# Splitting the output stores of the first two batches into two transfers each

## The chip, the cores and the metric

The kernel runs on one core of one Trainium2 chip. A core has a matrix engine (TensorE, PE in the profile), VectorE (DVE), ScalarE (ACT), GpSimd (POOL) and SyncE (SP). All of them work on the on-chip memory SBUF; TensorE's results go to banks of a second memory, PSUM. Transfers between SBUF and the device memory (DRAM) run on 16 DMA engines that the core's engines share; an engine only issues a transfer, in its own order of instructions, and goes on. Here SP issues the stores and the transposing transfers, and GpSimd issues nearly all loads. Completion of a transfer reaches those who wait for it through semaphores.

The metric is the device time in microseconds (us), the median of several runs.

## The reference

Attention through 32 memory slots per head, followed by a gated feed-forward block:

```python
a = softmax(phi, axis=2)                       # over the 576 positions, for each memory slot
k_m = einsum('bhsm,bhsd->bhmd', a, k)          # 32 x 64 for each batch and head
v_m = einsum('bhsm,bhsd->bhmd', a, v)
scores = (1 / sqrt(64)) * q @ k_m.transpose(0, 1, 3, 2)
attn_out = softmax(scores, axis=-1) @ v_m      # (8, 8, 576, 64)
x = attn_out.transpose(0, 2, 1, 3).reshape(4608, 512)
g = x @ w_gate                                 # 512 -> 1536
out = (g / (1 + exp(-g)) * (x @ w_val)) @ w_out    # 1536 -> 512, float32
```

There are 8 batches of 576 tokens. The output is 4608 x 512 floats, 9.44 MB.

## The kernel before

The kernel works batch by batch. For each batch, TensorE forms the sums over positions, the scores, the gate and value products (line 508), and the last product with `w_out` (line 719). That last product is computed with seven block products in place of eight (a scheme with sums of blocks). Each batch's first 512 tokens are treated as two sets of 256, the even and the odd ones of the output (`r` below), each in two groups `u` of 128 tokens. The remaining 64 tokens of every batch are collected and stored apart ("leftover").

The output view and the store. One call writes 256 tokens: partition `t` of the tile holds two rows of output, for `u` = 0 and 1.

```python
out_r = out.rearrange("(b t r) c -> b r t c", b=B, r=2)
...
def store_block(t_o, b, n, cols):
    nc.sync.dma_start(
        out=out_r[b, n, 0:256, cols].rearrange("(u t) c -> t u c", u=2), in_=t_o[:, :, cols]
    )
```

The tiles that are stored come from a pool with three buffers in rotation (tag `to`); a buffer can be written again when the store that read it has landed:

```python
work = ctx.enter_context(tc.tile_pool(name="work", bufs=3))
...
def add(out, home, other, free=False):              # line 749, VectorE
    nc.vector.tensor_tensor(out=out, in0=mine[home], in1=mine[other], op=ALU.add)
    if free:
        done(mine[home])                            # gives the PSUM bank back

def both(name, t0, cols):
    store_block(mine[name], b, t0 // 256, cols)

def c11():
    t = tile_of("o1", (128, 2, DM), tag="to")       # DM = 512 columns, lo and hi are its halves
    add(t[:, :, lo], "a", "p1", True)
    if end:                                         # end: the last batch alone
        both("o1", 0, lo)

def c22():
    t = tile_of("o2", (128, 2, DM), tag="to")
    add(t[:, :, hi], "s", "p5")

def c12():
    t = mine["o1"]
    add(t[:, :, hi], "c", "q6", True)
    both("o1", 0, hi if end else slice(0, DM))      # the even tokens' store

def c21():
    t = mine["o2"]
    copy("v" if end else "a", t[:, :, lo], mine["s"])
    done(mine["s"])
    both("o2", 256, slice(0, DM))                   # the odd tokens' store
```

So batches 0 to 6 have two stores of 512 KB each. Both halves of a tile are finished by one instruction, the addition in `c12` or the copy in `c21`.

On the same queue of SP are the transposing transfers of q and, for later batches, of the small matrices `t_bkv`:

```python
def load_qT(b):
    qTs[b] = att.tile([128, NS, 128], BF16, tag="qT", name="t_qT")
    nc.sync.dma_start_transpose(out=qTs[b], in_=qs[b])      # line 117
```

The loads of a batch are issued by GpSimd, three batches ahead (batch 4's once batch 1's last products are under way):

```python
def loads(b):
    if b < B:
        load_q(b)
        load_phi(b, nc.gpsimd)
        load_k(b)
        load_v(b)
```

The order of issue is fixed by hand. Batches 0 and 1 are the first two; their last products and their four stores come together, at the start of the loop over the batches from 2 on:

```python
(zero, ops0), (one, ops1) = products(0, ("c11",)), products(1, ("p1", "c11"))
...
run(zero[12:16] + zero[18:22] + kv[1:] + q2[2:] + zero[16:18] + zero[22:24])
...
loads(4)
backlog = one[6:12] + zero[36:] + one[12:36]
```

Of the kernel before, what the change touches and what calls it, by code (L numbers as in the profile page):

```python
# [14 lines left out]
def kernel(  # L15
# [19 lines left out]
    nc = tc.nc  # L35
# [29 lines left out]
    out_r = out.rearrange("(b t r) c -> b r t c", b=B, r=2)  # L65
# [604 lines left out]

    def store_block(t_o, b, n, cols):

        nc.sync.dma_start(
            out=out_r[b, n, 0:256, cols].rearrange("(u t) c -> t u c", u=2), in_=t_o[:, :, cols]
        )

    def store_leftover(t_o, b, cols, eng):

# [2 lines left out]
    def products(b, by_hand, quad=None):  # L681
# [71 lines left out]
        def both(name, t0, cols):  # L753
            store_block(mine[name], b, t0 // 256, cols)
# [354 lines left out]
```

The softmax here doesn't subtract the row's maximum and nothing guards it: scores larger than these inputs give would overflow.

## Time and profile before

| What | Number |
|---|---|
| median of three runs | 235.75 us (235.49 to 235.82) |
| span of the profiled execution | 233.8 us |
| granted TensorE clock, mean | 0.998 |
| TensorE busy | 224.5 us (96%) |
| VectorE, ScalarE, GpSimd busy | 78%, 74%, 60% |
| DMA | 36.84 MB in 36610 packets, mean 158 GB/s |
| stores of 512 KB, line 673 | 15, median 3.8 us from issue to landing |
| stores of 256 KB, line 673 | 2, median 2.2 us from issue to landing |

How to read it. Times are counted from the first instruction of the profiled execution. "Busy" is the time in which an engine works at an instruction; matmuls are pipelined, and a busy TensorE is not by that alone at its peak. The page cuts the span into 40 equal slices and gives each engine's busy share in tenths; the DMA row is the mean busy share of the 16 DMA engines. A row of "busy times by stage" has the stage, its length, then for each engine its busy time and in brackets its instructions (PE, weight loads, DVE, ACT, POOL), the granted clock, the DMA share and GB/s. An issue of a transfer in the SP queue is short; the time "to landing" runs from the issue to the last semaphore event of the transfer. The chain is the sequence of work that ended last, followed back from the end.

### The profile page before, as it was taken

The numbers are of one execution on the slowest core, as the hardware profiler recorded it, in microseconds if no ns is written. First come the engines' busy times: TensorE is split into PE (matmuls) and PEld (weight loads), VectorE is DVE, ScalarE is ACT, GpSimd is POOL, SyncE is SP. The second block draws the span as 40 slices with busy tenths as digits, with TensorE's granted clock in tenths as the row PEclk, the third lists the DMA queues.
The fourth block names the chain that finished last, engine by engine and source line by source line (L and its number), as shares of the span: only waits on it lengthen the run. The fifth ranks groups of instructions, "written<-read, shape, count | busy, mean of one in ns | idle before, by whom it ended". The sixth has DMA issues, their size and how long they took to land.

```text
span 233.8 us, 7201 instructions
## 1 busy us (share of the span) xinstructions
PE 224.5 (96%) x2825; PEld 169.9 (73%) x2825; DVE 183.2 (78%) x421; ACT 173.5 (74%) x369; POOL 140.6 (60%) x190
## 2 busy tenths in 40 slices
PE   7997899999999999999999999999999999999992
PEld 2554466778887776878788787877788778878881
DVE  4056799999966698989797767999799879977732
ACT  2759798988547889968896658968897789677220
POOL 8422536998199059665966688464745494039390
PEclk9999999999999999999999999999999999999999
DMA  6999999999995993999199946995024502201224
GB/s 213 210 210 206 200 206 207 231 236 266 205 241 134 261 251 47 231 227 151 35 259 212 190 128 121 254 217 94 15 78 110 106 0 94 90 35 57 62 76 136
DMA packets 36610, 36.84 MB, mean 158 GB/s; under 512 B 14560, under 2 KB 30944, under 8 KB 36576
## 3 DMA queue, kind: packets, MB, share of 16 engines
q0 software_dynamic: 16272, 22.42, 51.5%
q1 hardware_dynamic: 19536, 13.18, 23.6%
q10 hardware_dynamic: 768, 0.79, 1.1%
q8 instruction: 22, 0.36, 0.6%
q14 instruction: 12, 0.10, 0.1%
HBM read 42.47 MB, written 9.44 MB: 222 GB/s over the span
## 4 chain that ended last, share of the span: by engine, by line
PE 88%; DMA 7%; POOL 1%; ACT 1%; DVE 1%; issue 1%; POOLq 0%
PE p_v L508 21%; PE p_g L508 21%; PE p_os L719 20%; PE p_oc L719 10%; DMA t_kv<-in_v_dram 7%; PE p_u L465 5%; PE p_oa L719 5%; PE p_kv L230 2%; PE p_g L389 1%; POOL t_kv L99 1%; PE p_mT L318 1%; PE p_warm L866 1%; PE p_q L376 0%; POOL t_q L108 0%; DVE t_kT L332 0%
## 5 line engine op out<-in xcount | busy, mean ns | idle before, releaser
L531 DVE TENSOR_TENSOR t_h<-t_sg,p_v 128x288 bf16<-128x288 bf16 x192 | 81.9, 452 | 17.3 <-PE p_v L508 7.4
L508 PEld LDWEIGHTS <-t_U 128*128 128x128 bf16 x768 | 73.6, 98 | 23.2 <-issue 3.8
L525 ACT ACTIVATE t_sg<-p_g 128x288 bf16<-128x288 f32 x192 | 74.0, 424 | 17.8 <-PE p_g L508 11.5
L508 PE MATMUL p_g<-t_A,t_U 128*128 128x288 bf16 x384 | 77.1, 286 | 0.5 <-ACT t_U L487 0.5
L508 PE MATMUL p_v<-t_A,t_U 128*128 128x288 bf16 x384 | 77.2, 286 | 0.0
L719 PEld LDWEIGHTS <-t_S 128*128 128x128 bf16 x384 | 37.5, 98 | 4.5 <-issue 0.2
L596 POOL TENSOR_TENSOR t_S<-t_h 128x512 bf16<-128x512 bf16 x17 | 19.6, 1155 | 32.5 <-DVE t_h L531 30.4
L719 PEld LDWEIGHTS <-t_h 128*128 128x128 bf16 x288 | 27.1, 98 | 8.6 <-issue 5.0
L485 ACT CAST t_U<-p_u 128x512 bf16<-128x512 f32 x53 | 28.0, 607 | 6.6 <-PE p_u L465 6.6
L719 PE MATMUL p_os<-t_T,t_S 128*128 128x256 bf16 x192 | 23.7, 273 | 0.0
L553 POOL TENSOR_TENSOR t_S<-t_S,t_h 128x512 bf16<-128x512 bf16 x17 | 19.6, 1154 | 1.3
L553 POOL TENSOR_TENSOR t_S<-t_h,t_S 128x512 bf16<-128x512 bf16 x16 | 18.4, 1151 | 0.0
L553 POOL TENSOR_TENSOR t_S<-t_h 128x512 bf16<-128x512 bf16 x16 | 18.4, 1150 | 0.0
L465 PE MATMUL p_u<-W,t_kT 64*32 64x512 bf16 (+1 forms) x416 | 15.8, 364 | 0.6 <-DVE t_kT L332 0.6
L866 PE MATMUL p_warm<-bones 128*128 128x512 bf16 x44 | 13.8, 457 | 1.7 <-DVE bones L888 1.7
L719 PE MATMUL p_os<-t_T,t_h 128*128 128x256 bf16 x96 | 14.8, 273 | 0.0
L489 DVE CAST t_U<-p_u 128x512 bf16<-128x512 f32 x19 | 12.4, 684 | 1.9 <-PE p_u L465 1.9
L445 DVE TENSOR_TENSOR t_A<-t_E,t_lz 128x576 bf16<-128x576 bf16 x16 | 11.4, 739 | 0.7 <-ACT t_lz L421 0.7
L719 PE MATMUL p_oc<-t_T,t_S 128*128 128x256 bf16 x96 | 12.0, 273 | 0.0
L719 PE MATMUL p_oa<-WO,t_h 128*128 128x256 bf16 x96 | 11.8, 273 | 0.0
L719 PE MATMUL p_oc<-WO,t_S 128*128 128x256 bf16 x96 | 11.8, 273 | 0.0
L719 PE MATMUL p_os<-WO,t_h 128*128 128x256 bf16 x96 | 11.8, 273 | 0.0
(106 smaller groups left out, 308.8 us busy)
## 6 DMA issues: line engine op xcount, KB each, us to landing
out_dram<-t_o SPq DMA_DIRECT2D x15, 512.0 KB, 3.8
t_kv<-in_k_dram POOLq DMA_DIRECT2D x8, 576.0 KB, 10.2
t_q<-in_q_dram POOLq DMA_DIRECT2D x8, 576.0 KB, 8.6
t_kv<-in_v_dram POOLq DMA_DIRECT2D x8, 576.0 KB, 14.9
t_phi<-in_phi_dram POOLq DMA_DIRECT2D x6, 576.0 KB, 8.3
WO<-in_moe_w_out_dram POOLq DMA_DIRECT2D x3, 512.0 KB, 19.3
W<-in_moe_w_gate_dram POOLq DMA_DIRECT2D x2, 512.0 KB, 16.4
W<-in_moe_w_val_dram POOLq DMA_DIRECT2D x2, 512.0 KB, 16.2
```

Of the source, the lines that this page charges most:

```text
L230: nc.tensor.matmul(p[g][32 * i:32 * i + 32, 0:n], lhsT=phi_of(b, g, j, i), rhs=kvs[b][64 * g:64 * g + 64, w0:w1, i, j * D:(j + 1) * D], st ...
L445: nc.vector.tensor_tensor(out=a, in0=es.pop((b, g)), in1=lzs.pop((b, g)), op=ALU.mult)
L465: nc.tensor.matmul(p[g][32 * i:32 * i + 32, o:o + n], lhsT=kTs[b][64 * g:64 * g + 64, 2, 32 * i:32 * i + 32], rhs=w_part(w, c, i, g, halve ...
L485: nc.scalar.copy(out=t, in_=p)
L489: nc.vector.tensor_copy(out=t, in_=p)
L508: nc.tensor.matmul(p[:, 0:HALF], lhsT=Us[b, c, g][:, o // 2, which, 128 * (o % 2):128 * (o % 2 + 1)], rhs=atts[b, g][:, r], start=(g == 0) ...
L525: nc.scalar.activation(out=sg, in_=gate[:, 0:HALF], func=AF.Silu)
L531: nc.vector.tensor_tensor(out=dst, in0=sg, in1=val[:, 0:HALF], op=ALU.mult)
L553: eng.tensor_tensor(out=out, in0=x, in1=y, op=ALU.subtract)
L596: eng.tensor_tensor(out=t[:, 0], in0=A21, in1=A22, op=ALU.add)
L719: nc.tensor.matmul(mine[home][:, u], lhsT=lhs(c, m, u), rhs=rhs(c, m), start=fresh and u == 0, stop=(k == 5), skip_group_check=u == 1 or n ...
L866: nc.tensor.matmul(p[:, 0:128 * a], lhsT=bones, rhs=x.to_broadcast([128, a, 128]) if a > 1 else bones, start=True, stop=True,)
```

## The change

Stores of batches 0 and 1 are issued as two transfers of 128 tokens (256 KB) each, one for each `u`, in place of one of 256 tokens (512 KB). Batches 2 to 7 keep theirs. The tokens, the columns and the tiles are the same. It is meant to hand the DMA engines smaller pieces in the part of the kernel where loads for later batches run beside these stores.

```diff
     def store_block(t_o, b, n, cols):
 
-        nc.sync.dma_start(
-            out=out_r[b, n, 0:256, cols].rearrange("(u t) c -> t u c", u=2), in_=t_o[:, :, cols]
-        )
+        rows = out_r[b, n, 0:256, cols].rearrange("(u t) c -> t u c", u=2)
+        parts = [slice(u, u + 1) for u in range(2)] if b < 2 else [slice(0, 2)]
+        for u in parts:
+            nc.sync.dma_start(out=rows[:, u], in_=t_o[:, u, cols])
```

## The prediction

> **What bounds the kernel now.** I read the page first, then the engines' busy times by stage, then the chain that ended last around the four stores that the change splits, then the output tensor, the SP queue and the loads that share the DMA engines with those stores.
>
> From the page, the busy shares and the slices:
>
> ```profile
> PE 224.5 (96%) x2825; PEld 169.9 (73%) x2825; DVE 183.2 (78%) x421; ACT 173.5 (74%) x369; POOL 140.6 (60%) x190
> ...
> PE   7997899999999999999999999999999999999992
> ...
> DMA  6999999999995993999199946995024502201224
> ```
>
> TensorE is busy nearly always. The DMA row is just as full until about slice 23, so it could look like a second bound; that has to be decided stage by stage. The busy times by stage, from the first of these stores to near the end:
>
> ```profile
> 67.00:107.00 40.00, 39.95 (x565) 31.09 (x563) 34.24 (x75) 31.87 (x67) 25.21 (x33) 1.00 0.91 200
> 107.00:150.00 43.00, 42.97 (x522) 33.67 (x521) 34.45 (x78) 34.29 (x78) 33.09 (x44) 1.00 0.86 167
> 150.00:200.00 50.00, 50.00 (x656) 39.29 (x655) 44.43 (x98) 42.56 (x91) 28.54 (x40) 1.00 0.41 91
> 200.00:230.00 30.00, 29.34 (x267) 24.26 (x264) 20.92 (x45) 14.94 (x34) 15.55 (x22) 1.00 0.23 78
> ```
>
> After the length, the first column is TensorE's busy time. It is idle for 0.05, 0.03, 0.00 and 0.66 us: 0.74 us in all after the first store is issued. Busy matmuls overlap, so this alone doesn't show that they run at their rate. The chain in the same stage does:
>
> ```profile
> 65.62 1.31 PE p_os L719 x12
> ...
> 68.24 1.31 PE p_os L719 x12
> ...
> 77.07 0.49 PE p_g L508 x4
> ```
>
> Twelve products of 256 columns take 1.31 us, 109 ns each; four of 288 columns take 0.49 us, 122.5 ns each.
>
> **What the Trainium skill says.** "TensorE: Matmul & The Clock Gate", section Back-to-back issue gap, gives columns / 2.4 + 2.5 ns for a warm matmul by itself: 109.2 and 122.5 ns. The trace has the same two numbers, so TensorE is at that rate here, beside the stores. "DMA: Bandwidth & Descriptors", section Issuing engines are not separate DMA queues, says that transfers from all issuing engines run on the same 16 DMA engines and interleave. The trace agrees in part: during the third store the loads move too (below). The same page, section Anatomy of one DMA, puts a transfer issued by GpSimd at about 2.0 us plus bytes / 436 GB/s; my estimate from it is 3.2 us for 512 KB and 2.6 us for 256 KB. The quiet stores here, which SP issues, landed in 3.3 us (512 KB) and 2.2 us (256 KB, from the page's list of issues), so most of a small store is latency, and two issued together overlap it. "Perfetto Trace Analysis", section Identifying Dependency Chains, says that an instruction that waits on several others may get extra semaphore instructions ahead of it. The trace has 20 of them at the additions of line 749, mostly 21 to 50 ns.
>
> **The change, part by part.** Batches 0 and 1 each end with two stores (c12 and c21) of 128 partitions x 2 x 512 floats, 512 KB. The SP queue and the busy times around them:
>
> ```profile
> 61.32 5.97 SPq L117 DMA_TRANSPOSE t_qT<-t_q  x1
> 67.34 33.99 SPq L673 DMA_DIRECT2D out_dram<-t_o  x5
> 101.45 5.93 SPq L117 DMA_TRANSPOSE t_qT<-t_q  x1
> ```
>
> ```profile
> 71.10:74.30 3.20, 3.20 (x32) 2.87 (x31) 1.44 (x3) 3.18 (x4) 3.20 (x5) 1.00 0.61 172
> 74.30:83.20 8.90, 8.85 (x181) 6.02 (x179) 7.05 (x17) 7.08 (x18) 1.34 (x2) 1.00 0.98 237
> 83.20:90.00 6.80, 6.80 (x77) 4.94 (x75) 6.53 (x17) 5.91 (x16) 5.53 (x6) 1.00 0.96 193
> 90.00:92.00 2.00, 2.00 (x18) 1.47 (x16) 1.32 (x4) 2.00 (x6) 1.92 (x3) 1.00 0.00 0
> ```
>
> The 33.99 us is from the first of five issues to the end of the last, not busy time. The output tensor's own view, taken in narrow windows, has the issues at 67.34, 70.19, 74.30, 77.81 and 100.96 us, and 3.7, 3.3, 8.9, 8.9 and 6.4 us to landing. The first four are split; the fifth is of batch 2.
>
> Removed: 4 transfers of 512 KB. Added: 8 of 256 KB. Bytes stay at 4 x 512 KB = 2 MB, in runs of 2 KB, over the same 128 partitions. Only the order changes (all first halves, then all second halves, of each tile).
>
> 1. SP: one issue is 0.37 us, 0.58 us for the first. With the gap to the next instruction (0.05 to 0.12 us between the transposes and their neighbours) I take 0.45 us for an extra one: 4 x 0.45 = 1.8 us. SP's next other work is at 100.96 us, 22.8 us after the last of the four issues. On the path: 0.
>
> 2. Landing: both halves become ready together, since the addition or copy that finishes a tile writes both, so nothing starts earlier. The second half is issued 0.45 us later and moves half the bytes; the last byte lands, I estimate, between 0.3 us earlier and 0.6 us later than now. In the loaded stage (third and fourth store) the same bytes share the same engines, so I allow 1 us.
>
> 3. Buffers of t_o, three in rotation. The first store's buffer is rewritten by c22 of batch 1 at 74.86 us; its landing is 67.34 + 3.7 = 71.04, a slack of 3.8 us. The second's is rewritten at 96.58 and has landed at 70.19 + 3.3 = 73.5: 23 us. The third's at 100.85, landed at 74.30 + 8.9 = 83.2: 17 us. None of this is eaten by 1 us. The rewriting instruction has two completions to await instead of one: 4 x 21 to 50 ns = 0.1 to 0.2 us on VectorE, which has 40 - 34.24 = 5.8 us idle in this stage. On the path: 0.
>
> 4. Loads of batch 4, issued by GpSimd from 72.83 us, collide with the third and fourth store. They land at 79 (q), 81 (phi), 87 (k) and 90 us (v), from their issue plus 6.2, 7.9, 12.8 and 15.0 us. First uses: the phi exponential at 97.3, q's transpose at 101.45, the k and v sums at 103.87. The least slack is 103.87 - 89.9 = 14 us. The row 90 to 92 settles it: DMA share 0.00. The engines have drained everything before batch 5's loads begin at 92.01, so a different order before 90 us can't reach later transfers unless it lasts 2 us longer.
>
> Sum on the path: 0 + 0 + 0 + 0. Predicted 235.75 us, the time before.
>
> **The rivals.** First, a gain: smaller transfers let the loads through sooner, or free t_o sooner. For it speaks that the DMA engines are 98% busy from 74.3 to 83.2 us, and that a store takes 8.9 us there against 3.3 in quiet. Against it: TensorE waits for no transfer in this stage and idles 0.05 us in 40. Even if all its later idle time went, the time would be 235.75 - 0.74 = 235.0 us, 0.3%.
>
> Second, a loss at the buffer with the least slack: if the first store's second half landed 3.8 us later than now, c22 of batch 1 would stall VectorE, the PSUM bank p_os would come free late, and TensorE would wait. A doubled latency (3.7 to 7.4 us) still ends at 74.74, just ahead of 74.86. A stall of 1 to 2 us would make 236.7 to 237.7 us. Nothing in the trace suggests such a delay: the DMA share from 71.1 to 74.3 us is 0.61, so there was room.
>
> Third, a loss through the DMA engines: eight completions in place of four lengthen the drain past 92 us and push batch 5's loads. That needs 2 us or more, and these have slack of their own. I give it less weight; it would make some tenths of a us, about 236.0.
>
> **Range and chances.** The three runs before spread over 0.33 us (235.49 to 235.82). Shifts in which queue is served first can, by my judgement, move a program by as much again, so I take 235.3 to 236.3 us, with more room above, since splitting can only add instructions and the gain is capped at 0.74. Two per cent is 4.7 us: a gain of that size exceeds all idle time that TensorE has left after the change, and a loss would need several of the slacks above to fail at once. Chances: faster 0.01, same 0.98, slower 0.01.
>
> **What would show it.** In the changed profile I expect: 21 issues of line 673 in place of 17, the pairs about 0.45 us apart; halves landing in 2 to 3.5 us for the first two tiles and within about 1 us of 8.9 for the other two; the addition at 74.86 us and the transpose at 101.45 within 0.2 us of their places; TensorE busy 39.9 of 40 us from 67 to 107; DMA share near 0.00 from 90 to 92. The prediction is wrong if VectorE waits for out_dram at line 749, if the sums of batch 4 wait for a load, if the drain lasts beyond 92 us, or if matmuls lose their 109 and 122.5 ns while the stores run.

## The result, and the profile after

The changed kernel takes 235.02 us (234.82 to 235.12), against 235.78 us (235.49 to 236.11) for the kernel before, measured beside it: a ratio of 0.9966, 95% interval 0.9953 to 0.9978. It is faster by 0.76 us, 0.34%. The prediction was 235.75 us, in a range of 235.3 to 236.3; the result lies below it.

The page of the kernel after: busy shares and slices.

```profile
PE 223.6 (96%) x2825; PEld 169.7 (73%) x2825; DVE 183.2 (79%) x421; ACT 173.6 (74%) x369; POOL 140.6 (60%) x190
...
PE   7987899999999999999999999999999999999993
...
DMA  6999999999995992999099945995022702102125
```

TensorE is busy 0.9 us less, but the first slices already differ, in its warm-up. The busy times by stage of the kernel after, with the stages of the prediction:

```profile
67.00:107.00 40.00, 39.95 (x564) 31.09 (x563) 34.22 (x75) 31.91 (x67) 25.14 (x33) 1.00 0.92 200
107.00:150.00 43.00, 42.97 (x523) 33.67 (x521) 34.44 (x78) 34.30 (x77) 33.13 (x44) 1.00 0.86 167
150.00:200.00 50.00, 50.00 (x656) 39.31 (x654) 44.42 (x98) 42.55 (x91) 28.46 (x40) 1.00 0.42 91
200.00:230.00 30.00, 29.29 (x266) 24.22 (x264) 20.85 (x45) 14.89 (x34) 15.56 (x22) 1.00 0.23 78
```

The first three rows have TensorE's numbers of before to the hundredth. So has the chain, three entries of which stand here: 109 and 122.5 ns for each matmul, and each entry 0.05 or 0.06 us earlier than before.

```profile
65.57 1.31 PE p_os L720 x12
...
68.19 1.31 PE p_os L720 x12
...
77.01 0.49 PE p_g L508 x4
```

Compared matmul by matmul over the whole trace, TensorE is ahead by 0.06 us at 25.9 us and by 0.05 at 226.4, and by 0.05 or 0.06 everywhere between. The 67 to 90 us with the split stores win and lose nothing.

The SP queue of the kernel after, and the stages around the stores:

```profile
61.40 5.99 SPq L117 DMA_TRANSPOSE t_qT<-t_q  x1
67.44 33.84 SPq L676 DMA_DIRECT2D out_dram<-t_o  x9
101.39 6.26 SPq L117 DMA_TRANSPOSE t_qT<-t_q  x1
```

```profile
71.10:74.30 3.20, 3.20 (x32) 2.88 (x30) 1.44 (x3) 3.18 (x4) 3.20 (x5) 1.00 0.62 169
74.30:83.20 8.90, 8.85 (x181) 6.02 (x180) 7.04 (x17) 7.08 (x18) 1.27 (x2) 1.00 0.99 240
83.20:90.00 6.80, 6.80 (x76) 4.94 (x75) 6.52 (x17) 5.91 (x16) 5.58 (x6) 1.00 0.93 187
90.00:92.00 2.00, 2.00 (x17) 1.47 (x16) 1.32 (x4) 2.00 (x6) 1.92 (x4) 1.00 0.00 0
```

There are nine issues in place of five, and the engines have again drained by 90 us. Where, then, are the 0.7 us of the span? After all engines have stopped computing. The last stages of the kernel before:

```profile
229.00:230.00 1.00, 0.34 (x4) 0.06 (x1) 0.51 (x2) 0.00 (x0) 0.00 (x0) 1.00 0.34 80
230.00:233.80 3.80, 0.00 (x0) 0.00 (x0) 0.00 (x0) 0.00 (x0) 0.00 (x0) 0.86 0.37 86
```

and of the kernel after:

```profile
229.00:230.00 1.00, 0.29 (x3) 0.01 (x1) 0.45 (x2) 0.00 (x0) 0.00 (x0) 1.00 0.38 92
230.00:233.10 3.10, 0.00 (x0) 0.00 (x0) 0.00 (x0) 0.00 (x0) 0.00 (x0) 1.00 0.43 101
```

From VectorE's last copy on, both kernels have the same work, and it takes 3.80 us in place of 4.44, 0.64 us less. With the 0.05 us that TensorE was ahead this is the whole difference of the two spans, 233.82 and 233.13 us. What SP waited for from 229 us to the end, before and after:

```profile
SPq L1104 <- DMA out_dram<-t_q: 1.6, 2, 1.0
SPq L1104 <- PEq L1104: 0.7, 2, 0.5
```

```profile
SPq L1105 <- DMA out_dram<-t_q: 0.9, 2, 0.7
SPq L1105 <- PEq L1105: 0.7, 2, 0.5
```

At the end SP waits, one after the other, until every transfer of the kernel has landed; then come drains (instructions without a transfer) and a barrier, at which all engines meet. The SP and ACT transfers (ACT issues one early load, and three stores of 64 tokens near the end) take turns on eight semaphores, and SP's closing instructions wait for these in a fixed order. There are 44 such transfers before and 48 after. So the last one signals on the fourth semaphore before and on the eighth after. Here are the closing instructions in the two traces: their number in SP's own stream, counted from 0, the start in us, the time in ns since the instruction before ended, and which of the eight semaphores the wait holds. (The first line holds semaphores of GpSimd's loads alone.)

```
before                               after
72 230.377   46  loads               78 230.340   44  loads
73 231.385  980  first               79 230.828  460  first
74 231.446   33  second              80 230.911   55  second
75 232.088  614  third  (last, ACT)  81 230.985   47  third
76 232.183   67  fourth (last, SP)   82 231.047   34  fourth
77 232.258   47  fifth               83 231.361  286  fifth
78 232.328   42  sixth               84 231.423   34  sixth
79 232.815  459  seventh             85 232.148  697  seventh (last, ACT)
80 232.899   56  eighth              86 232.209   33  eighth  (last, SP)
81 232.969   42  drain               87 232.274   37  drain
```

"Last" marks the semaphores on which the kernel's very last two stores signal. ACT's lands last, at 232.07 us before and 232.13 after; SP's lands at 231.8 in both. Two things differ. Before, four more waits follow these two, 0.07 to 0.08 us apart but for the pause, although what they wait for has landed; after, none does. And ahead of instruction 79, in both, SP pauses for 0.46 us although what it waits for has long come: before, this stands behind the last landing; after, six instructions earlier in the ending, where SP has to wait for landings anyhow. From the wait for SP's last store, at which both have landed, to the drain it is 232.969 - 232.183 = 0.786 us before and 232.274 - 232.209 = 0.065 us after: 0.72 us. The pause is 0.459 - 0.047 = 0.41 of it, the four waits the other 0.31. Counted from VectorE's last copy, that wait is reached 0.08 us later than before, which leaves the 0.64 us.

That gave the theory for the experiments. A: the time is won in SP's closing waits, by where the last stores' semaphores stand and where the pause falls; that stores were split is beside the point. B, the change's own purpose: smaller stores let the loads pass.

### The profile page after: what moved, and what is told of

Same layout as the page of the kernel before. It is cut to its first block, busy times and chain, and to the rows that moved or that the text cites. A ratio compares the mean times of both kernels' runs of the same rounds, so it can differ in the third digit from the quotient of the medians.

```text
span 233.1 us, 7210 instructions
## 1 busy us (share of the span) xinstructions
PE 223.6 (96%) x2825; PEld 169.7 (73%) x2825; DVE 183.2 (79%) x421; ACT 173.6 (74%) x369; POOL 140.6 (60%) x190
## 4 chain that ended last, share of the span: by engine, by line
PE 88%; DMA 7%; POOL 1%; ACT 1%; DVE 1%; issue 1%; POOLq 0%
PE p_v L508 21%; PE p_g L508 21%; PE p_os L720 21%; PE p_oc L720 10%; DMA t_kv<-in_v_dram 7%; PE p_u L465 5%; PE p_oa L720 5%; PE p_kv L230 2%; PE p_g L389 1%; POOL t_kv L99 1%; PE p_mT L318 1%; PE p_warm L867 1%; PE p_q L376 0%; POOL t_q L108 0%; DVE t_kT L332 0%
## 5 line engine op out<-in xcount | busy, mean ns | idle before, releaser
L867 PE MATMUL p_warm<-bones 128*128 128x512 bf16 x44 | 13.0, 434 | 1.7 <-DVE bones L889 1.7
```

The lines of the kernel that those rows point to most:

```text
L867: nc.tensor.matmul(p[:, 0:128 * a], lhsT=bones, rhs=x.to_broadcast([128, a, 128]) if a > 1 else bones, start=True, stop=True,)
```

## The experiments

"Beside" is the kernel before, run on the same chip; "tail" is the time from the start of VectorE's last copy to the end, in the trace.

| Run | us | Beside | Ratio (95%) | Tail, us |
|---|---|---|---|---|
| before | 235.78 | | | 4.44 |
| the change | 235.02 | 235.78 | 0.9966 (0.9953 to 0.9978) | 3.80 |
| e1 small loads on SP | 235.19 | 235.85 | 0.9976 (0.9969 to 0.9983) | 3.80 |
| e2 two drains | 235.70 | 235.85 | 0.9992 (0.9984 to 1.0) | 4.44 |
| e3 six drains | 235.46 | 235.85 | 0.9984 (0.9977 to 0.999) | 3.98 |
| e4 small loads on ACT | 235.10 | 235.85 | 0.9966 (0.9953 to 0.9979) | 3.70 |
| e5 split 2, 3 | 235.05 | 235.89 | 0.9967 (0.9954 to 0.9979) | 3.78 |
| e6 split 0 to 3 | 235.57 | 235.89 | 0.9984 (0.9976 to 0.9993) | 4.18 |
| e7 change and small loads | 235.45 | 235.89 | 0.9982 (0.9975 to 0.9988) | 4.10 |
| e8 e4, one less on SP | 235.31 | 235.89 | 0.9979 (0.9969 to 0.9989) | 4.17 |
| e9 e4, two less on SP | 236.33 | 235.92 | 1.002 (1.0013 to 1.0027) | 4.26 |
| e10 e4 again | 234.93 | 235.92 | 0.9958 (0.9945 to 0.9971) | 3.71 |
| e11 e8 again | 235.41 | 235.92 | 0.9973 (0.9963 to 0.9983) | 4.17 |

**Four more transfers, no store split (e1).**

```diff
+    def tick(eng):
+        t = consts.tile([128, 4], FP32, ...)          # nobody reads it
+        eng.dma_start(out=t, in_=phi[0, 0, 0:128, 0:4])
 ...
     def store_block(t_o, b, n, cols):
         nc.sync.dma_start(...)                          # as before
+        if b < 2:
+            tick(nc.sync)
```

> The stores of batches 0 and 1 stay whole; after each of the four, SP issues a load of 2 KB that nobody reads. Theory A (the time is won at the end: SP's closing waits for the eight completion semaphores of the SP and ACT transfers come in a fixed order; four more transfers move the last stores from the third and fourth of these semaphores to the last two, and six more instructions of SP move its pause of 0.46 us from after the last landing to before it): 235.0 us, and SP's pause stays ahead of its 80th instruction, now the first but one of the closing waits. Theory B (smaller stores beside the loads win the time): 235.75 us.

235.19 us: a gain of 0.66 us, nearly that of the change, with work added and no store changed. The tail is 3.80 us as in the change, and SP's ending looks the same, pause ahead of its instruction 79 included. B falls as the main cause.

**The length of SP's stream alone (e2, e3).** Drains use no transfer, so the semaphores stay where they were. Six is the number of instructions by which the change lengthens SP's stream: four issues and two semaphore instructions.

```diff
     load_phi(0, nc.sync)
+    for _ in range(6):           # e2: 2
+        nc.sync.drain()
```

> The kernel before, with two more instructions of SP (drains, no transfer) right after its first load. Theory A: the pause of 0.46 us moves ahead by two waits, to the one on the fifth semaphore, still behind the last landing (fourth): 235.75 us, no change. A rival A2 (any instruction more on SP helps, in proportion): a third of the whole gain with six, 235.6 us. Theory B: 235.75 us.

> The same with six drains, as many instructions as the change adds to SP, and no transfer. Theory A: the pause stands ahead of the first of the eight waits, before the last landing, and is hidden; the order of the semaphores stays, so four waits of about 0.07 us follow the last landing as before: gain 0.41 us, 235.35 us. Theory B: 235.75 us.

Two drains give 0.15 us, which is hardly told from nothing (the interval reaches 1.0), and leave the tail at 4.44 us; six give 0.39 us and a tail of 3.98. In e2's trace the pause of 0.474 us is ahead of the fifth semaphore's wait, behind the last landing; in e3's no pause is left behind it, and four quick waits follow, as foreseen. So it isn't that each instruction helps: what counts is on which side of the last landing the pause falls.

**The semaphores alone (e4).** Four small loads on ACT, late, leave SP's stream as long as before.

```diff
         if last:
+            for _ in range(4):
+                tick(nc.scalar)
             rest, rest_ops = products(b, (), 1)
```

> The kernel before, with four loads of 2 KB issued by ACT in the last batch. SP's stream keeps its length, so its pause stays ahead of the same closing wait (the seventh semaphore); but the last stores now signal on the last two semaphores. Theory A: the pause falls before the last landing and is hidden, and no wait follows it: 235.05 us. If only the number of SP's instructions counted: 235.75 us. Theory B: 235.75 us.

235.10 us, and 234.93 the second time (e10): the whole gain. SP's instruction 79 is the seventh wait, as before, but now the last landing is what it waits for, and the pause is lost in that wait: the gap ahead of it is 0.619 us, against 0.697 ahead of the same wait in the changed kernel, where no pause is due.

**Splitting elsewhere, and more of it (e5, e6, e7).**

```diff
-        parts = [slice(u, u + 1) for u in range(2)] if b < 2 else [slice(0, 2)]
+        parts = [slice(u, u + 1) for u in range(2)] if b in (2, 3) else [slice(0, 2)]   # e5
+        parts = [slice(u, u + 1) for u in range(2)] if b < 4 else [slice(0, 2)]         # e6
```

e7 is the changed kernel with e1's four loads.

> The same splitting, but of the stores of batches 2 and 3 in place of 0 and 1: four more transfers, four more instructions of SP. Theory A (the gain lies in SP's closing waits: which semaphores the last stores signal on, and where SP's pause of 0.46 us falls): the last two semaphores, and the pause ahead of the third of the eight closing waits, before the last landing: 235.05 us, as for the change itself. Theory B (smaller stores beside the loads of batches 3 and 4 win the time, at 67 to 90 us): nothing is split there, so 235.8 us.

> The change doubled: the stores of batches 0 to 3 are split, eight more transfers. Eight is the number of the semaphores, so the last stores are back on the third and fourth: four waits of 0.07 us follow the last landing again. SP's pause is still away from the closing waits, now at the last store but one of SP, which it can delay by some 0.1 to 0.2 us at the end. Theory A: the gain shrinks to 0.25 to 0.45 us, 235.45 us. Theory B: twice the gain, or at least all of it: 234.3 to 235.05 us.

> The changed kernel, with the four loads of 2 KB of the first experiment added on SP. Stores of batches 0 and 1 are split as in the change, but with eight more transfers in all the last stores are back on the third and fourth semaphore, and the pause falls at the last store but one of SP. Theory A: 235.45 us, part of the gain lost. Theory B: 235.05 us, the gain stays.

Splitting the stores of batches 2 and 3 gives the same as those of 0 and 1. Doubling the change doesn't double the gain but leaves less than half of it, 0.32 us (e6); adding four loads to the change leaves 0.44 us (e7): with eight more transfers the last stores are on the third and fourth semaphore again. In e6 the pause stands ahead of the issue of SP's last store but one (0.461 us), and SP's last issue begins at 230.10 us, against 229.83 in the change, with its tail 0.38 us longer.

**The pause put back (e8 to e11).** e4's loads, and one or two leftover stores near 140 us moved from SP to ACT, so that SP has one or two instructions fewer.

```diff
-            engs = (nc.sync, nc.scalar if end and name != "c11" else nc.sync)
+            engs = (nc.sync, nc.scalar if (end and name != "c11")
+                    or (not end and name == "c12") else nc.sync)        # e9: in ("c12", "c21")
```

> The fourth experiment (four small loads on ACT, last stores on the last two semaphores), and one store of 64 tokens of batch 0 to 3 issued by ACT in place of SP, near 140 us, so that SP has one instruction fewer. SP's pause then stands ahead of the very last closing wait, behind the landing that ends the one before it. Theory A: the pause is exposed again, 235.1 + 0.41 = 235.5 us. Theory B, or a theory in which only the order of the semaphores counts: 235.1 us.

> As the eighth experiment, with a second store of 64 tokens of batches 0 to 3 issued by ACT, so that SP has two instructions fewer than in the fourth. Theory A: SP's pause stands ahead of its first closing drain, behind all eight waits, and is exposed: 235.5 us, 0.4 us more than the fourth experiment, and the last landing is no later. In the trace the stretch from the last matmul to the end is 0.4 to 0.5 us longer than there. If only the order of the semaphores counts: 235.1 us. Theory B: 235.8 us.

> The fourth experiment once more, beside the other two on one chip: 235.1 us, pause hidden.

> The eighth experiment once more, beside the other two on one chip: 235.5 us by theory A, pause exposed ahead of the last wait; 235.1 us if only the order of the semaphores counts.

e8 came out between the two expectations, so e4 and e8 were run again on one chip: 234.93 us (e10) and 235.41 us (e11), 0.48 us apart, with A's 0.41 foreseen. The end of e10's and then of e11's trace, by the span and the last copy:

```profile
core 0 of [0], span 233.3 us
...
229.56 0.42 DVE L332 COPY t_q<-p_os 128x256 f32<-128x256 f32 x1 [0.30 <-PE p_os L726]
```

```profile
core 0 of [0], span 233.2 us
...
229.07 0.42 DVE L332 COPY t_q<-p_os 128x256 f32<-128x256 f32 x1 [0.29 <-PE p_os L726]
```

The profiled execution of e11 reached its last copy 0.48 us sooner and yet ended at nearly the same time: 3.71 us of tail in e10, 4.17 in e11. In e11's, SP's pause (0.473 us) is ahead of the eighth wait, behind the landing that ends the seventh.

The two parts of the gain can now be told apart by the tail. With neither moved it is 4.44 us (before); with the pause alone moved ahead of the last landing 3.98 (e3); with the last stores alone on the last semaphores 4.17 (e11); with both 3.71 (e10). Alone they save 0.46 and 0.27 us, together 0.73, their sum. In time e11 is 0.51 us faster than before, more than its tail accounts for; in its trace TensorE was 0.31 us ahead at 25.9 us already.

e9 missed its expected 235.5 by 0.8 us. Its pause is where A puts it (0.479 us ahead of the first drain, tail 4.26 us), 0.55 us of tail more than e10. But the second moved store has a price of its own: TensorE falls behind by 0.6 us between 141.6 and 149.3 us and doesn't catch up, in e9 alone. The trace fits a delay by the issue itself: ACT issues the second moved store from 141.87 to 142.37 us, and its next pair of activations begins at 142.41, against 141.45 in e10. No run tests it. e9's time therefore says little about the pause; its trace agrees with it.

No version beats the change beyond its uncertainty: e4 and e5 are level with it.

## Why the prediction was wrong

**What bounds the kernel** was right: matmuls kept their 109 and 122.5 ns, and no experiment but e9 moved TensorE's course after the first 26 us by more than 0.12 us. None of the four signs of being wrong appeared: they all belong to the stages before 107 us, and what went wrong lies behind 230.

**Step 1, SP.** The cost of an extra issue was sized about right: the added issues took 0.42, 0.44, 0.64 and 0.45 us without the gap behind them, against 0.45 with it. But six instructions came to SP's stream, not four: two semaphore instructions follow the third and the fourth pair. The step failed in "On the path: 0". I asked only when SP was wanted next, at 100.96 us, and not whether SP is on the path at the end. It is: in the last 3.8 us, when no engine computes any more. There SP's stream is the critical path, and a longer stream with other semaphores changed it. The missing term is -0.72 us in the two traces: -0.41 by the pause (e3 gained 0.39 by it alone) and -0.31 by the waits after the last landing.

**Step 2, landing.** The halves of the first tile landed at 67.44 + 3.0 = 70.4 and 68.06 + 4.0 = 72.1 us, 1.1 us after the whole one before, more than the 0.6 allowed. Those of the second landed at 72.7 and 73.3 (before 73.5), of the third at 81.7 and 83.3 (83.2), of the fourth at 84.8 and 86.6 (86.7): within the allowed 1 us for the last bytes, though the first halves took 7.5 and 7.0 us, well under 8.9. That most of a small store is latency doesn't follow from 3.3 us for 512 KB and 2.2 for 256 KB: 256 KB more cost 1.1 us, so about half of the 2.2 is left for it.

**Step 3, buffers.** Right. The slack of 3.8 us became 74.81 - 72.1 = 2.7 us; the addition at 74.86 us stands at 74.81, with the whole of TensorE's course. Two semaphore instructions were added at that line (22 for 20); the prediction had allowed for four waits.

**Step 4, loads.** Right: the row 90 to 92 us again has a DMA share of 0.00.

**The rivals.** The first, a gain by the loads or buffers, didn't happen; e1 and e5 give the gain without it. Its cap of 0.74 us, TensorE's idle time up to 230 us, resembles the measured 0.76 by accident: none of that idle time was won, and the cap left out the stage after 230 us, in which TensorE is not busy at all. That stage was not in my table, which ended at 230.00, and the chain ended at VectorE's last copy, so I never asked what the remaining 3.8 us were.

**The range** allowed for noise on both sides, with more room above on the ground that splitting can only add instructions. Here six added instructions made the kernel faster (e3). With the closing waits written down beforehand one would have found the semaphores' order from the count of transfers; the pause's place could be read from the trace of before, as the gap of 459 ns ahead of SP's instruction 79.

## What to carry to other kernels

A table of stages has to reach the end of the span. Here, after the last arithmetic, the stream of SP that waits for all transfers was the critical path, and drains added to it near its start (e3), or loads added on another engine (e4), shifted what stood last there. Before crediting a change of some tenths of a per cent to its purpose, add the same number of idle instructions, or of transfers that do nothing, and see whether they give the same.

## What the runs showed of the hardware

SP pauses 0.46 to 0.48 us ahead of instruction 79 of its stream wherever this pause can be seen by itself: ahead of a wait, of a drain (e9), of a store (e6). It moves when instructions are added or taken away, and stays at that number. In each of the thirteen traces a transfer of 8 KB on the queue that the page calls "instruction" begins 1.1 to 1.3 us after instruction 78 ends. So it does in e3, e4 and e10, where the pause is hidden in a wait (1.18, 1.08 and 1.10 us). It begins at 233.4 us before, in the window from 233 to 233.5, and at 231.6 us after, in that from 231.5 to 232:

```profile
q14 instruction: 1, 0.01, 6.2%
```

```profile
q14 instruction: 1, 0.01, 6.3%
```

So the pause looks like the crossing into another block of SP's program; this is inferred from number and time, not shown.

The times of one kernel differ by up to 1.1 us (e1: 234.72 to 235.83). In the traces, the differences before SP's ending arise mostly at the start: at 25.9 us TensorE is between 0.54 us ahead of the kernel before and 0.22 us behind it, and each trace keeps its difference to 0.03 us for the next 100 us, whatever was done to the stores. Later it changes in two: by 0.12 us in e10, between 130 and 138 us, and by 0.6 in e9.
